# Output pieces of a soft-MoE kernel through two DMA queues: the column halves alternate between SyncE and GpSimd

## The chip, the cores and the metric

The kernel runs on one core of a Trainium2 chip. The metric is the device time of one execution in microseconds (us), as the median over several runs. A core has five engines with instruction streams of their own: TensorE (PE, with its weight loads as PEld), VectorE (DVE), ScalarE (ACT), GpSimd (POOL) and SyncE (SP). Data between HBM and the on-chip memory goes through 16 DMA engines, which all DMA queues share. A profile is taken of one execution and has times in us from the start of its span.

## The reference

Sliding-window causal attention (window 64) feeds a soft mixture of experts with 8 experts of 4 slots. There are 8 batches of 576 tokens, 8 heads of 64, so D = 512 and the output has 4608 rows of 512 float32 values.

```python
scores = scale * np.matmul(q, k.transpose(0, 1, 3, 2))      # q, k, v: (8, 8, 576, 64)
scores = np.where((rel >= 0) & (rel < 64), scores, -1e9)
x = softmax(scores) @ v                                      # -> (4608, 512)
logits = x @ phi                                             # (4608, 32)
slot_input = softmax(logits, axis=0).T @ x                   # 32 slots
slot_out[e] = np.maximum(slot_input[e] @ w1[e], 0) @ w2[e]   # F = 1024
out = softmax(logits, axis=1) @ slot_out                     # (4608, 512) float32
```

## The kernel before

For the first 150 us the kernel works through 32 pairs of heads in a software pipeline written out by hand: scores, exponentials, the product with V, the router's logits, and running sums of the slots' inputs. Loads of q, k, v and of the experts' weights are issued by GpSimd, which also converts them from float32 to float16 on the way; they go through queue q0 of the profile ("software_dynamic"). SP issues the first few loads and all outputs, through queue q1 ("hardware_dynamic").

From 151 us on the experts run. `first` and `turn_hidden` make the hidden values, `second` and `second_last` multiply by the second weights, one half of the 512 columns at a time (`DH` = 256): `osb` has its columns 0 to 255 at 159.9 us and its columns 256 to 511 at 165.1 us. The last weights come in by column halves as well (`load_half`, lines 148 to 156).

The output is 8 x 576 rows. Two batches make a group `k` (0 to 3) of 1,152 rows, which is laid out as 128 partitions of `NE` = 9 neighbouring rows each (`e` = 0 to 8). `give(k, e0, ne, c0, nc_)` (lines 883 to 902) makes one piece, `ne` rows per partition and `nc_` columns from `c0`. It multiplies the spread weights `ct4[k]` by the slots' outputs `osb` into a PSUM tile `cp` (line 893), divides by the sums while it copies to SBUF, by DVE (line 898) or ACT (line 900) in turn, and issues one DMA to HBM (line 902). A whole-row piece has 3 x 512 neighbouring values in a partition, one packet of 6 KB; a piece of a column half has `ne` packets of 1 KB in each partition.

The pieces lie in seven SBUF buffers `obs` that once held the first experts' weights. A piece takes the next buffer in turn, so piece i can be written only after piece i-7 has landed. The order of pieces is written out in lines 909 to 938: the two halves of group 0 and of the first three rows of group 1 first (8 pieces of 256, 256, 640, 384, 256, 384, 512 and 384 KB), then 8 pieces of whole rows with 768 KB each. Every engine executes its own instructions in the order written, so a DMA that waits for its data holds up the ones behind it on the same engine.

Of the kernel before, what the change touches and what calls it, by code (L numbers as in the profile page):

```python
# [18 lines left out]
def kernel(  # L19
# [10 lines left out]
    nc = tc.nc  # L30
# [115 lines left out]
    DH = D // 2  # L146
# [507 lines left out]
    def spread(b, copy, rp=None):  # L654
        if rp is None:
            rp = psr.tile([128, 1024], FP32, name="rp", tag="rp")
        for t in range(5):
            w = 128 if t < 4 else 64
            nc.tensor.matmul(rp[:, 128 * t:128 * t + w], ss4[:, min(t, 3), :],
                             ct_all[:, b, 128 * (t // 4):128 * (t // 4) + w], start=True, stop=True,  # L660
                             skip_group_check=True)
        copy(out=ct4[b // 2][:, :, 64 * (b % 2):64 * (b % 2) + 64],
             in_=rp[:, 0:S].rearrange("p (x e) -> p e x", e=NE))
# [170 lines left out]
    def second(d, g, js=range(4)):  # L834
        for fc in range(NFC):
            for j in js:
                nc.tensor.matmul(ops[d][32 * j:32 * j + 32, 0:DH], hT[g][:, fc, 32 * j:32 * j + 32],
                                 w2_at(4 * g + j, d, fc), start=(g == 0 and fc == 0), stop=False,
                                 skip_group_check=True)
# [40 lines left out]

    turn, piece = 0, 0

    def give(k, e0, ne, c0, nc_):
        nonlocal turn, piece
        ov = out[2 * S * k:2 * S * k + 2 * S, :].rearrange("(p e) d -> p e d", e=NE)
        ob = obs[piece % NRES][:, 0:ne * nc_].rearrange("p (e d) -> p e d", d=nc_)
        piece += 1
        n1 = 512 // nc_
        for i0 in range(0, ne, n1):
            n_ = min(n1, ne - i0)  # L890
            cp = pst.tile([128, n1, nc_], FP32, name="cp", tag="cp")
            for i in range(n_):
                nc.tensor.matmul(cp[:, i, :], ct4[k][:, e0 + i0 + i, :], osb[:, c0:c0 + nc_],  # L893
                                 start=True, stop=True, skip_group_check=True)
            for i in range(n_):
                rc = rcs[:, k, e0 + i0 + i:e0 + i0 + i + 1]
                if turn % 2:
                    nc.vector.tensor_scalar(out=ob[:, i0 + i, :], in0=cp[:, i, :], scalar1=rc, scalar2=None, op0=ALU.mult)  # L898
                else:
                    nc.scalar.activation(ob[:, i0 + i, :], cp[:, i, :], AF.Copy, scale=rc)  # L900
            turn += 1
        nc.sync.dma_start(out=ov[:, e0:e0 + ne, c0:c0 + nc_], in_=ob)

    def spread_product(b):
        rp = psr.tile([128, 1024], FP32, name="rp", tag="rp")
# [5 lines left out]
    late = []  # L911
    spread_product(3)
    give(0, 0, 2, 0, DH)
    give(0, 2, 2, 0, DH)
    dve(out=late[0][0], in_=late[0][1])
    give(0, 4, 5, 0, DH)
    second(1, 0)
    second(1, 1, (0, 1))
    sums(1)
# [1 line left out]
    second_last(1)  # L921
    act(out=osb[:, DH:D], in_=ops[1][:, 0:DH])
    give(0, 0, 2, DH, DH)
    give(0, 2, 3, DH, DH)
    give(0, 5, 4, DH, DH)
    spread(4, act)
    give(1, 0, 3, DH, DH)
    spread(5, dve)
    for k in range(1, B // 2):
        for e0 in range(3 if k == 1 else 0, NE, 3):  # L930
# [36 lines left out]
```

## Time and profile before

| | |
|---|---|
| Median of 3 runs | 190.65 us (190.38 to 191.93) |
| The profiled execution | 192.31 us, span 190.5 us |
| Busy share of the span | PE 85%, PEld 64%, DVE 75%, ACT 76%, POOL 52% |
| Output | 9.44 MB in 16 DMAs, all issued by SP |
| First and last output issue | 161.3 us, 178.3 us |

PE is the busiest engine over the whole span. In the last fifth the picture is another one: the compute engines end near 177.6 us while the DMA engines work on. In the stretch tables, the columns behind an engine's busy time give its instructions (x), then come the clock granted to TensorE, the DMA share (the mean of the 16 engines; it can pass 1 where packets overlap) and GB/s. GB/s counts what is written, so a load that converts to float16 shows half of what it reads. In the DMA views each queue has a line with packets, MB and the time its packets took as a share of 16 engines' time.

### The profile page before, as it was taken

Reading aid. Unit: us, or ns where it says so; the run is one execution under the profiler, and the core shown is the slowest. Engines: PE = TensorE matmul, PEld = TensorE weight load, DVE = VectorE, ACT = ScalarE, POOL = GpSimd, SP = SyncE. Lnnn points to the kernel's source line nnn. Section 1 sums busy time; section 2 is a strip of 40 time slices with the busy share of each in tenths; the row PEclk is TensorE's granted clock in tenths of the full one; section 3 lists DMA queues with packets and bytes.
Section 4 is the critical chain, followed back from the end, with each engine's and each line's share of the span. In section 5 each row is a group of like instructions: output and inputs, shape, how many; then the busy total and the mean of one; then the engine's idle time right before and its main releaser. Section 6 shows DMA issues by size and latency. Waiting matters only on the chain.

```text
span 190.5 us, 7073 instructions
## 1 busy us (share of the span) xinstructions
PE 162.3 (85%) x3039; PEld 121.6 (64%) x3039; DVE 142.7 (75%) x354; ACT 145.1 (76%) x267; POOL 98.8 (52%) x123
## 2 busy tenths in 40 slices
PE   5987999999999999999999899999988898878100
PEld 1566878877777777777777787776774466643000
DVE  6778686897778789788888988888886555699400
ACT  6558979989889899888998898988588257499200
POOL 7956937274696644973984828736844160000000
PEclk9999999999999999999999999999999999999955
DMA  6999999999999999999999999999999999999993
GB/s 171 207 185 189 224 177 220 179 224 178 186 222 178 216 187 185 211 194 182 214 187 202 202 184 203 196 200 201 214 212 212 201 196 154 310 341 415 413 410 125
DMA packets 62303, 41.48 MB, mean 218 GB/s; under 512 B 38848, under 2 KB 58304, under 8 KB 61376
## 3 DMA queue, kind: packets, MB, share of 16 engines
q0 software_dynamic: 56560, 30.35, 115.4%
q1 hardware_dynamic: 5712, 10.68, 15.8%
q8 instruction: 24, 0.39, 0.7%
q14 instruction: 7, 0.06, 0.1%
HBM read 61.93 MB, written 9.44 MB: 375 GB/s over the span
## 4 chain that ended last, share of the span: by engine, by line
PE 44%; DVE 26%; issue 7%; ACT 7%; DMA 4%; POOL 4%; DVEq 0%; ACTq 0%; POOLq 0%
DVE m L353 7%; PE a_m L346 5%; PE a_m L349 5%; DVE x_b L415 4%; PE a_q L316 4%; PE a_s L372 3%; PE a_v L405 3%; PE a_s L375 3%; DMA out_dram<-w 3%; PE a_k L316 2%; DVE acc L526 2%; DVE kT L324 2%; PE a_k L429 2%; PE ha L816 2%; DVE rt L367 2%
## 5 line engine op out<-in xcount | busy, mean ns | idle before, releaser
L336 ACT ACTIVATE qb<-a_q 64x576 f16<-64x576 f16 x63 | 40.6, 645 | 6.9 <-PE a_q L316 5.4
L353 DVE TENSOR_REDUCE m<-a_m 128x8 f16<-128x1024 f32 x32 | 39.1, 1223 | 1.9 <-PE a_m L349 1.0
L381 ACT ACTIVATE pt<-a_s 128x1024 f16<-128x1024 f32 x32 | 32.8, 1025 | 6.8 <-PE a_s L375 5.5
L180 POOL COPY v<-v 64x1152 f16<-64x1152 f16 x16 | 18.3, 1142 | 33.3 <-DMA v<-in_v_dram 32.0
L415 DVE TENSOR_TENSOR x_b<-a_v,rc 128x640 f16<-128x640 f32 x31 | 25.6, 825 | 1.1
L349 PEld LDWEIGHTS <-qb 128*128 128x128 f16 x256 | 17.3, 99 | 8.5 <-ACT qb L336 0.8
L349 PE MATMUL a_m<-kT,qb 128*128 128x128 f16 x256 | 20.0, 222 | 0.3 <-ACT qb L336 0.3
L375 PEld LDWEIGHTS <-lh 128*128 128x128 f16 x288 | 18.7, 98 | 2.0 <-issue 1.7
L173 POOL DMA_DIRECT2D v<-in_v_dram x16 | 20.0, 1247 | 0.0
L346 PE MATMUL a_m<-wm,ident_h 128*128 128x512 f16 x64 | 19.8, 391 | 0.2 <-DVE m L353 0.2
L372 PEld LDWEIGHTS <-kT 128*128 128x128 f16 x288 | 18.6, 98 | 1.6 <-issue 1.4
L433 ACT COPY xt<-a_k 128x576 f16<-128x576 f16 x28 | 17.9, 640 | 2.2 <-PE a_k L429 0.9
L372 PE MATMUL a_s<-qb,kT 128*128 128x128 f16 x256 | 19.5, 219 | 0.0
L375 PE MATMUL a_s<-rt,lh 128*128 128x128 f16 x256 | 19.5, 219 | 0.0
L182 POOL COPY v<-v 64x1088 f16<-64x1088 f16 (+1 forms) x16 | 17.9, 1119 | 0.8
L405 PE MATMUL a_v<-v,pt 128*64 128x65 f16 x558 | 15.8, 196 | 2.5 <-DVE m L363 1.1
L367 DVE CAST rt<-a_v 9x128 f16<-9x128 f32 x30 | 8.7, 289 | 10.8 <-PE a_v L366 10.5
L405 PEld LDWEIGHTS <-pt 128*64 128x64 f16 x576 | 13.6, 110 | 4.9 <-issue 1.8
L79 POOL DMA_DIRECT2D ks<-in_k_dram x15 | 10.7, 714 | 11.0 <-DMA w<-in_moe_w_dram 3.9
L327 ACT ACTIVATE kT<-a_k 128x576 f16<-128x576 f16 x24 | 15.7, 654 | 0.8 <-PE a_k L316 0.8
L316 PE MATMUL a_q<-ident_h,qs 96*64 96x96 f16 x384 | 15.2, 211 | 1.2 <-DVE a_q L225 1.0
L898 DVE TENSOR_SCALAR w<-cp,rcs 128x256 f32<-128x256 f32 (+1 forms) x24 | 13.5, 611 | 2.1 <-PE cp L893 1.7
(183 smaller groups left out, 332.8 us busy)
## 6 DMA issues: line engine op xcount, KB each, us to landing
w<-in_moe_w_dram POOLq DMA_DIRECT2D x13, 1024.0 KB, 16.8
out_dram<-w SPq DMA_DIRECT2D x8, 768.0 KB, 7.7
v<-in_v_dram POOLq DMA_DIRECT2D x16, 288.0 KB, 12.5
ks<-in_k_dram POOLq DMA_DIRECT2D x15, 288.0 KB, 15.4
qs<-in_q_dram POOLq DMA_DIRECT2D x15, 288.0 KB, 12.6
out_dram<-w SPq DMA_DIRECT2D x3, 384.0 KB, 3.5
w1h<-in_moe_w_dram POOLq DMA_DIRECT2D x4, 256.0 KB, 16.1
w<-in_moe_w_dram POOLq DMA_DIRECT2D x4, 256.0 KB, 14.9
```

The source lines that it names most:

```text
L173: nc.gpsimd.dma_start(out=v1s[b % 2][:, c, 0:Dh], in_=v[b].rearrange("h s d -> (h s) d").rearrange("(c p) d -> p c d", p=128)[:, c, :])
L180: nc.gpsimd.tensor_copy(out=v2[64:128, c0:c1, 0:Dh], in_=v1[0:64, c0:c1, 0:Dh])
L316: nc.tensor.transpose(tq[64 * hf:64 * hf + 64, RP * r:RP * r + RP], src[0:RP, h + hf, Dh * r:Dh * r + Dh], ident_h[0:RP, 0:RP])
L336: nc.scalar.activation(qbs[p % NQ][h, :, hf, :], turned(a_qh)[h], AF.Copy, scale=QKS)
L346: nc.tensor.matmul(a_m[:, j, :], ident_h[:, :], wm[:, j:j + 4, :].rearrange("p c x -> p (c x)"), start=True, stop=False, skip_group_check= ...
L349: nc.tensor.matmul(a_m[:, i // 4, 128 * (i % 4):128 * (i % 4) + 128], qblock(p, i), kwindow(p, i), start=False, stop=True, skip_group_chec ...
L353: nc.vector.reduce_max(ms[p % 2][:, 64:72].rearrange("p (l c) -> p l c", l=2), a_m[:, :, :].rearrange("p l (c x) -> p l c x", x=128), axis ...
L372: nc.tensor.matmul(at(i), kwindow(p, i), qblock(p, i), start=(i % 4 == 0), stop=False, skip_group_check=True)
L375: nc.tensor.matmul(at(i), lh[:, i, :], rt[:, :], start=False, stop=True, skip_group_check=True)
L381: nc.scalar.activation(st_pt(p)[:, 0:8, :].rearrange("p i x -> p (i x)"), a_s[:, :, :], AF.Exp, scale=XS)
L405: nc.tensor.matmul(a_v[r0:r0 + 64, hf, 65 * (i // 2):65 * (i // 2) + 65], pt[:, i, 64 * hf:64 * hf + 64], rhs, start=True, stop=True, skip ...
L415: nc.vector.tensor_tensor(out=xbs[b][:, :, 128 * hp:128 * hp + 128].rearrange("p c (l d) -> p l c d", l=2), in0=avv[:, :, :, 0:64], in1=rc ...
```

## The change

`give` gets a parameter for the engine that issues its DMA, SP unless told otherwise. Of the pieces of column halves, every second one goes through GpSimd. The piece of five rows (group 0, rows 4 to 8, first columns) becomes two pieces of 2 and 3 rows, so there are 9 pieces of column halves in place of 8: five through SP and four through GpSimd. The piece of group 1 in the first columns, which the diff does not show, stays on SP. All pieces of whole rows stay on SP.

```diff
-    def give(k, e0, ne, c0, nc_):
+    def give(k, e0, ne, c0, nc_, queue=nc.sync):
...
-        nc.sync.dma_start(out=ov[:, e0:e0 + ne, c0:c0 + nc_], in_=ob)
+        queue.dma_start(out=ov[:, e0:e0 + ne, c0:c0 + nc_], in_=ob)
...
     give(0, 0, 2, 0, DH)
-    give(0, 2, 2, 0, DH)
+    give(0, 2, 2, 0, DH, nc.gpsimd)
     dve(out=late[0][0], in_=late[0][1])
-    give(0, 4, 5, 0, DH)
+    give(0, 4, 2, 0, DH)
+    give(0, 6, 3, 0, DH, nc.gpsimd)
     second(1, 0)
...
     give(0, 0, 2, DH, DH)
-    give(0, 2, 3, DH, DH)
+    give(0, 2, 3, DH, DH, nc.gpsimd)
     give(0, 5, 4, DH, DH)
     spread(4, act)
-    give(1, 0, 3, DH, DH)
+    give(1, 0, 3, DH, DH, nc.gpsimd)
     spread(5, dve)
```

## The prediction

> **What bounds the kernel now.** I read the page's slices first, then the stretch from the first output piece to the end by stretches, then that stretch's DMA queues, then the lines of the issuing engines. The slices show the DMA engines at 9 to the end while every compute engine falls off after slice 36:
>
> ```profile
> PE   5987999999999999999999899999988898878100
> ...
> DMA  6999999999999999999999999999999999999993
> ```
>
> ```profile
> core 0: us, PE busy (x) PEld busy (x) DVE busy (x) ACT busy (x) POOL busy (x), PEclk, DMA share, GB/s
> ...
> 163.75:164.00 0.25, 0.25 (x3) 0.04 (x1) 0.22 (x1) 0.00 (x0) 0.00 (x0) 1.00 0.70 215
> 164.00:165.75 1.75, 1.28 (x23) 1.07 (x23) 1.11 (x3) 0.86 (x3) 0.00 (x0) 1.00 1.05 354
> 165.75:166.00 0.25, 0.25 (x3) 0.10 (x1) 0.25 (x2) 0.25 (x1) 0.00 (x0) 1.00 0.69 225
> 167.00:167.50 0.50, 0.41 (x5) 0.21 (x3) 0.50 (x2) 0.50 (x2) 0.00 (x0) 1.00 0.82 275
> ...
> 172.50:181.00 8.50, 4.18 (x27) 1.45 (x25) 5.57 (x10) 4.52 (x8) 0.00 (x0) 1.00 1.02 413
> ...
> 187.25:189.00 1.75, 0.00 (x0) 0.00 (x0) 0.00 (x0) 0.00 (x0) 0.00 (x0) 0.50 0.06 25
> ```
>
> The last two columns are read here. A full DMA share goes with 354 GB/s while the column halves go out (rows of 1 KB) and with 413 GB/s for whole rows (6 KB). Over 16 engines that is 46.3 ns for a 1 KB packet and 238 ns for a 6 KB one (39.7 ns per KB). Compute ends at 177.6, yet data moves until 189: the tail is DMA-bound. The engines run dry three times before 167.5, for (0.30 + 0.31) x 0.25 + 0.18 x 0.5 = 0.24 us of a mean engine. And the last row is one engine of 16 (0.06): fifteen are done at 187.25, one works 1.75 us longer. Why it lags stands in the DMA views of 163 to 164.5 and of 181 to 183, one line of each:
>
> ```profile
> q8 instruction: 1, 0.02, 4.0%
> ```
>
> ```profile
> q8 instruction: 1, 0.02, 2.9%
> ```
>
> Two instruction fetches, 4.0% of 16 x 1.5 and 2.9% of 16 x 2 engine-us, are 0.96 and 0.93 us, 1.89 together, about the lag less the gaps that the others had. That both fell on the same engine is inferred from that sum. I call it the late engine: **it sets the end**, and what the other fifteen lose costs nothing until they are later than it is.
>
> **Issue, and who could be late.** For the 16 issues, line 902:
>
> ```profile
> L902 SPq DMA_DIRECT2D out_dram<-w x16: 332/404/1133, 161.3 to 178.3; - x16
> ...
> DMA to landing us min/median/max: 2.8/4.6/11.1
> ```
>
> Asked by single microseconds they start at 161.3, 161.8, 163.0, 165.0, 166.4, 166.9, 167.8 and 168.6 (halves), then 169.8 to 178.3 (whole rows). The last lands 11.1 us after its issue, so supply is some 8 us ahead at the end: a whole piece is 786 KB, 1.9 us at 413 GB/s. SP's 0.4 us a piece therefore buys nothing late. GpSimd is idle in this stretch; its last work is
>
> ```profile
> 155.85 0.51 POOL L488 TENSOR_TENSOR lh<-lh,nm 128x192 f32<-128x192 f32 x1 [0.21 <-DVE nm L483]
> ```
>
> **The change, part by part.** In the built program's order every matmul and eviction keeps its place and engine (the split piece had evictions of 2, 2 and 1 rows, and has them still). Only buffer numbers shift by one after the split. SP has 13 output DMAs in place of 16; GpSimd gets four at its end: pieces of 2, 3, 3 and 3 rows, 11 x 128 = 1,408 packets of 1 KB, 88 to a DMA engine. Nothing stands behind them on GpSimd; their own semaphores were last used by loads issued before 146, landed by 159.
>
> *Issue time.* SP drops four issues and gains one: 3 x 0.4 = 1.2 us of an engine that waits anyway. A GpSimd issue of 512 rows (line 155) takes
>
> ```profile
> L155 POOL DMA_DIRECT2D w2h<-in_moe_w_dram x4: 742/742/742, 143.9 to 153.9; - x4
> ```
>
> so 4 x 0.74 us on an idle engine. Both cost 0, covered by the data in flight.
>
> *Time per packet.* No row shows a GpSimd store. Nearest by what moves is SP's own 1 KB store, 46.3 ns. GpSimd's loads of 1 KB rows (halved to 512 B) at 153 to 157 were 1,574 packets less 48 small ones in 4 us: 41.9 ns. Their time in flight, 144.8% of 64 engine-us over 1,574, is 58.9 ns. On 88 packets the bounds are -4.4 x 88 = -0.39 us and +12.6 x 88 = +1.11 us. I take the store's row: 0.
>
> *Delay to the first packet.* SP: issue at 161.27, first packet just after 162.1, 0.9 us. GpSimd on an empty ring is seen once, at the kernel's start: issue at 2.05, only SP's packets until 5.3, first two of its own by 5.6, some 3.3 us. Between 0.9 and 3.3 I take 3.3, since SP's ring was then as full as now. The second piece (evicted at 161.45) would start at 164.8 instead of 163, the fourth (162.9) at 166.2. SP's two pieces of 2 rows, the second now issued near 162.1, last until about 163.8 as before. The gap there grows from 0.25 to 1 us, and 0.3 us follow before 165.95. A common engine loses (1.0 + 0.3) - 0.24, about 1.1 us: it ends near 188.3, not 187.25. But the late engine spends one gap on its first fetch (it lags 0.96 us there) and starves for 0.1 to 0.3 us at most. With 0.9 us instead, it starves for nothing. I take **+0.1 us**. Were that cover gone (no fetch there), the 1.1 us would all show.
>
> *Buffers.* With seven buffers, piece i (from 0) waits for the landing of i-7. Pieces 13 and 15 (k=2 e0=6, k=3 e0=3) now wait for GpSimd's third and fourth. Issued at 166.9 and 168.6, with 3.3 us of delay and 1.1 us of data each, these land near 172 and 174; the two pieces are issued at 174.9 and 177.0 in the trace, after 1.4 us of evictions, so their buffers are wanted near 173.5 and 175.5. Cost 0, if the rings share so that 1.1 us of data takes no more than a few.
>
> *Sum.* The profiled execution: 192.31 us, span 190.5, 1.8 around it. 192.31 + 0 + 0 + 0.1 + 0 = 192.4. It is 1.66 above the median of the runs shown, so **190.8 us** against 190.65.
>
> The Trainium skill, "DMA: Bandwidth & Descriptors", section "Issuing engines are not separate DMA queues", says that DMAs from sync, scalar and GpSimd end on the same 16 engines and that more issuers save issue time alone. By that rule the sum is the same, 0 for bandwidth; the shares of 1.05 and 1.02 with one issuer agree.
>
> **Rivals.**
>
> *Slower: the last GpSimd piece lands too late.* Its 24 packets per engine meet SP's 6 KB packets. Shared packet by packet, each costs 46 + 238 = 284 ns. For: at 5 to 9 us, where both rings were full, GpSimd moved 625 packets and SP 675, near one to one. Against: at 162.25 to 163.25 GpSimd's load tail ran on at 145 packets beside SP's 219, about the rate it had alone on the few engines that still held it. One to one, the third piece (from 170.2) has some 16 packets beside 6 KB ones, 4.5 us, and ends at 175; the fourth needs 24 x 0.284 = 6.8 us more: 182, on the late engine 183 to 184. Who waits is piece 15: eviction of three rows on two engines, 2 x 0.68, then 0.9 us to data. The late engine has finished piece 14 at 189.0 - 2 x 1.9 = 185.2, so the landing decides from 182.9 on, and then us for us: 0.1 to 1.1 late, and with the third piece's own delay to piece 13 up to 3. I price it at +1.7: **192.4 us**.
>
> The Trainium skill, "DMA: Bandwidth & Descriptors", section "Queues, rings and completion order", has each DMA engine go round its rings, a packet of about 9 to 17 descriptors at a time. By that an estimate is 24 descriptors in two or three turns, each behind a turn of SP's of up to a whole piece, 1.9 us: 5 to 7 us, much as one to one. It speaks for this rival, and so do the counts at 5 to 9 us; those at 162.25 do not.
>
> *Dearer packets.* GpSimd's store packets cost their time in flight: +1.1 on the late engine, with 0.3 of starving: **192.1 us**. For: the 58.9 ns. Against: they overlap, 41.9 ns apart.
>
> *Faster: two rings fill each other's gaps.* All 24 x 8 = 192 packets of 1 KB on an engine fall from 46.3 to 39.7 ns: -1.27 us, **189.4 us**. For: the share of 1.19 with both rings at 162.25 to 163.25. Against: that stretch moved 364 packets in a us, 44 ns each, little better than one ring.
>
> **How the numbers follow.** Forecast 0.50, late landing 0.25, dearer packets 0.12, filled gaps 0.13. The likeliest's own range is 190.2 to 191.6. A change of 1%, 1.9 us, is about what a measurement of this kernel can tell from none. Slower by more: half of the late landing, a third of the dearer packets, and some for both together with a cost that no row shows, 0.25. Faster by more needs -1.9, past the -1.27 and -0.39 worked out; I leave 0.12, mostly for a late engine that lags less. Same: 0.63. The range is 189.3 to 193.2.
>
> **What would show it.** Right: data until 188.8 to 189.4, one engine alone for the last 0.6 us or more, SP's half-row rate still near 354, GpSimd's pieces landing within 6 us, a hole in the DMA share near 164 to 165. Wrong: GpSimd's fourth piece landing after 182, with DVE or ACT waiting for it at line 898 or 900 and DMA share under 1 at 183 to 186; or more than 370 GB/s with both rings at work.

## The result and the profile after

Over 22 runs each, the changed kernel took 191.75 us in the median (191.19 to 193.16), the kernel before 190.88 us (190.38 to 192.11). The ratio is 1.0052 with a 95% interval of 1.0031 to 1.0072: **slower by 0.5%**, about 0.9 us. The forecast was 190.8, and its range (189.3 to 193.2) holds the time, which lies just above the likeliest outcome's own range (190.2 to 191.6). But the loss is clear of noise, and it is most of an amount that the prediction had worked out and then set aside. The profiled execution has a span of 191.1 us.

Counted from the first output issue, the compute engines did what they did before, to within 0.2 us; the two profiles of the kernel before (e12 below is the second) differ by as much. What changed is the DMA stretch between the first output issue (161.0) and 172. Here it is in stretches (the last two columns are DMA share and GB/s):

```profile
core 0: us, PE busy (x) PEld busy (x) DVE busy (x) ACT busy (x) POOL busy (x), PEclk, DMA share, GB/s
163.75:164.25 0.50, 0.50 (x13) 0.32 (x13) 0.43 (x2) 0.39 (x1) 0.23 (x1) 1.00 0.96 326
164.25:164.75 0.50, 0.30 (x7) 0.19 (x4) 0.44 (x2) 0.21 (x2) 0.00 (x0) 1.00 0.75 252
164.75:166.75 2.00, 1.28 (x12) 1.01 (x12) 1.27 (x3) 1.31 (x4) 0.00 (x0) 1.00 1.01 366
166.75:167.25 0.50, 0.50 (x9) 0.40 (x7) 0.44 (x2) 0.50 (x3) 0.00 (x0) 1.00 0.47 156
167.25:168.00 0.75, 0.28 (x5) 0.17 (x4) 0.75 (x3) 0.75 (x2) 0.72 (x1) 1.00 1.01 344
168.00:168.75 0.75, 0.75 (x8) 0.27 (x5) 0.55 (x2) 0.72 (x3) 0.06 (x1) 1.00 0.37 128
168.75:171.25 2.50, 2.05 (x19) 0.94 (x19) 2.50 (x6) 2.32 (x4) 0.76 (x1) 1.00 1.00 333
171.25:171.75 0.50, 0.50 (x8) 0.33 (x6) 0.50 (x1) 0.42 (x1) 0.00 (x0) 1.00 0.94 309
174.00:187.00 13.00, 2.83 (x14) 0.73 (x10) 4.01 (x7) 3.28 (x6) 0.00 (x0) 0.78 1.01 412
...
188.00:189.25 1.25, 0.00 (x0) 0.00 (x0) 0.00 (x0) 0.00 (x0) 0.00 (x0) 0.50 0.07 29
```

The full stretches run at the rates of before: 412 GB/s for whole rows (413 before), 333 to 366 for column halves. But there are holes: 0.25 x 0.5 + 0.53 x 0.5 + 0.63 x 0.75 + 0.06 x 0.5 = 0.89 us of a mean engine, against 0.24 before. The largest, at 168.0 to 168.75, did not exist. Before, the same stretch was full:

```profile
168.00:168.75 0.75, 0.75 (x8) 0.33 (x6) 0.55 (x2) 0.75 (x3) 0.00 (x0) 1.00 1.03 335
```

GpSimd's four issues show why (its timeline from 160 on):

```profile
161.49 0.73 POOL L902 DMA_DIRECT2D out_dram<-w  x1 [5.42 <-DVE w L898]
163.22 0.77 POOL L902 DMA_DIRECT2D out_dram<-w  x1 [0.99 <-DVE w L898]
167.28 0.78 POOL L902 DMA_DIRECT2D out_dram<-w  x1 [3.30 <-ACT w L900]
168.81 0.76 POOL L902 DMA_DIRECT2D out_dram<-w  x1 [0.75 <-ACT w L900]
```

The third is issued at 167.28, and at 168.5 to 168.65 queue q0 moves its first packet, some 1.4 us after the issue (1.36 to 1.37 in each of the four traces that have this hole: this one, e5, e7 and e9); SP's first output packet came 0.9 us after its issue. On top, the issue itself is late. Before, SP issued this piece 5.6 us after the first output issue; GpSimd does it 6.3 us after. Of these 0.6 us, 0.2 are a later compute (the next piece of SP is 0.2 late as well), the rest is GpSimd's own: it issues 0.3 us (first and fourth piece) to 0.6 us (second and third) after the last eviction of the piece, SP within 0.1 us when it is free.

One thing of the queue table was in no account: GpSimd does not send the rows as SP does.

```profile
q0 software_dynamic: 56976, 31.79, 117.2%
q1 hardware_dynamic: 4256, 9.24, 13.6%
```

Before:

```profile
q0 software_dynamic: 56560, 30.35, 115.4%
q1 hardware_dynamic: 5712, 10.68, 15.8%
```

SP has lost 1,456, which is 1,408 rows and 3 x 16 completions. GpSimd has gained 416, which is 4 x 16 completions and 352 packets: four rows of 1 KB in each, 1.44 MB in all.

### The profile page after: what moved, and what is told of

Same layout as the page of the kernel before. It is cut to its first block, busy times and chain, and to the rows that moved or that the text cites. A ratio compares the mean times of both kernels' runs of the same rounds, so it can differ in the third digit from the quotient of the medians.

```text
span 191.1 us, 7073 instructions
## 1 busy us (share of the span) xinstructions
PE 162.1 (85%) x3039; PEld 121.4 (64%) x3039; DVE 143.1 (75%) x354; ACT 145.0 (76%) x267; POOL 101.2 (53%) x127
## 4 chain that ended last, share of the span: by engine, by line
PE 47%; DVE 33%; ACT 7%; issue 4%; DMA 2%; DVEq 0%; SPq 0%; ACTq 0%
DVE m L353 10%; PE a_m L346 6%; PE a_m L349 5%; DVE x_b L415 5%; PE a_s L372 4%; PE a_s L375 4%; PE a_v L405 3%; PE a_q L316 3%; DVE acc L526 3%; PE a_k L429 2%; DVE kT L324 2%; DVE rt L367 2%; DMA w<-in_q_dram 2%; PE ha L816 2%; PE op L837 2%
## 5 line engine op out<-in xcount | busy, mean ns | idle before, releaser
L405 PE MATMUL a_v<-v,pt 128*64 128x65 f16 x558 | 15.3, 196 | 2.2 <-DVE m L363 1.1
```

Source lines behind the costliest of these rows:

```text
L405: nc.tensor.matmul(a_v[r0:r0 + 64, hf, 65 * (i // 2):65 * (i // 2) + 65], pt[:, i, 64 * hf:64 * hf + 64], rhs, start=True, stop=True, skip ...
```

## The experiments

**Theory A**: GpSimd's pieces reach the DMA engines later than SP's; where little else waits the engines run dry, and a DMA-bound tail never makes that up. **Theory B**: DMA time itself grows, by a second ring or by GpSimd's packets. **Theory C**: the split costs it. Each experiment but e12, a single run, was timed beside the kernel before. In the table, "gap" is summed over the quarter microseconds from 1 to 25 us after the first output issue with a DMA share under 0.95 (what is missing to 1; a packet counts in each quarter with the part that lies in it), and "end" is when, after that issue, the share falls under a half. Both come from one profile of each kernel.

| Kernel | Ratio to before (95%) | Gap, us | End, us |
|---|---|---|---|
| before, two profiles | 1 | 0.23; 0.26 | 26.0; 26.25 |
| changed, first profile | 1.0052 (1.0031 to 1.0072) | 1.04 | 26.75 |
| e5, changed again | 1.0044 (1.0008 to 1.0079) | 1.07 | 26.75 |
| e1, split, all on SP | 0.9988 (0.9953 to 1.0022) | 0.49 | 26.0 |
| e2, ACT for GpSimd | 1.0002 (0.9971 to 1.0033) | 0.36 | 26.25 |
| e3, before + 768 KB | 1.0076 (1.0049 to 1.0103) | 0.24 | 28.0 |
| e4, changed + 768 KB | 1.0098 (1.0065 to 1.0132) | 0.07 | 27.75 |
| e6, first two on GpSimd | 0.9988 (0.9958 to 1.0018) | 0.37 | 26.0 |
| e7, last two on GpSimd | 1.0104 (1.0058 to 1.0150) | 1.16 | 26.75 |
| e8, whole rows on GpSimd | 1.0020 (0.9987 to 1.0054) | 0.41 | 26.25 |
| e9, the third alone | 1.0042 (1.0009 to 1.0075) | 0.97 | 26.5 |
| e10, the fourth alone | 1.0011 (0.9985 to 1.0036) | 0.37 | 26.0 |
| e11, all but the third | 1.0019 (0.9992 to 1.0046) | 0.42 | 26.25 |

**e1: the split alone.**

```diff
-    give(0, 2, 2, 0, DH, nc.gpsimd)
+    give(0, 2, 2, 0, DH)
...
-    give(0, 6, 3, 0, DH, nc.gpsimd)
+    give(0, 6, 3, 0, DH)
...
```

and the other two back on SP in the same way.

> The changed kernel with its split piece, but every piece issued by SP. Theory A (GpSimd's pieces reach the DMA engines later than SP's, and the gaps that this opens before 169 us, while there is nothing else to send, are never made up): the split alone opens no gap and closes the one at 163.75, so 0 to -0.3 us against before (190.6 to 190.9). Theory B (a second ring, or GpSimd's packets, cost DMA time): also 0, since neither is used. Theory C (the split, with one DMA more and the buffers moved by one, costs the time): +0.6 to +0.9 us, as the change.

Measured: 191.27 us in the median, 191.04 before, ratio 0.9988 (0.9953 to 1.0022). Theory C falls: its +0.6 us would be 1.003. One expectation missed: the split does open a gap, 0.34 us at 5.25 to 6.5 us after the first issue (0.10 and 0.16 in the two profiles of before), but the end and the time do not show it.

**e2: ACT in GpSimd's place.**

```diff
-    give(0, 2, 2, 0, DH, nc.gpsimd)
+    give(0, 2, 2, 0, DH, nc.scalar)
...
```

> The changed kernel with ACT in GpSimd's place: the same four pieces, a second ring, but issued by an engine like SP. Theory A: first packets about 0.9 us after the issue as with SP, no new gap beyond what ACT's four issues of 0.4 us take from its evictions: -0.2 to +0.4 us against before. Theory B as a cost of two rings: +0.6 to +0.9 us. Theory B as a cost of GpSimd's packets alone: as A.

Measured: 190.94 us, ratio 1.0002 (0.9971 to 1.0033). The four pieces went through a ring of their own, q10, as packets of 1 KB, and nothing was lost. So a second ring costs nothing that shows here, and wins nothing either. What is left of theory B is GpSimd's packets.

**e3 and e4: a cushion of work.** Both kernels get the same addition behind the first piece:

```diff
     give(0, 0, 2, 0, DH)
+    o3 = out[6 * S:8 * S, :].rearrange("(p e) d -> p e d", e=NE)
+    for e in range(3):
+        nc.sync.dma_start(out=o3[:, e, :], in_=w1_t[e, 0][:, 3, :].bitcast(FP32))
```

> The kernel before with 768 KB more to send: right behind the first piece SP issues three DMAs of 256 KB from SBUF to output rows that later pieces write anew. Both theories: 1.9 us more of DMA work at 413 GB/s, less the 0.24 us of gaps that it fills: +1.6 to +1.9 us against before, with no share under 0.95 between 163 and 187 us.

> The changed kernel with the same 768 KB behind its first piece, so that the DMA engines have work while GpSimd's pieces are on their way. Theory A: the gaps (1.03 us of a mean engine in the changed kernel's trace, against 0.24 before) are filled, and the difference to the kernel before with the same addition is within 0.3 us. Theory B (DMA time itself has grown): the difference stays at +0.6 to +0.9 us.

Measured: 192.92 and 192.89 us, ratios 1.0076 and 1.0098. The two intervals overlap widely (the ratios differ by 0.2%, 0.4 us, with some 0.8 us of uncertainty), so the times alone do not decide. The traces speak for theory A. In e4, the stretch with the three holes is full:

```profile
163.00:169.00 6.00, 4.42 (x56) 2.83 (x55) 4.48 (x11) 4.27 (x10) 1.86 (x3) 1.00 1.04 362
...
168.00:168.75 0.75, 0.75 (x6) 0.15 (x3) 0.60 (x1) 0.72 (x3) 0.06 (x1) 1.00 1.02 354
```

and its engines end 27.75 us after the first issue, 28.0 in e3. With the holes filled, 1.44 MB through GpSimd take no more DMA time than through SP. The 1.5 to 2 us that both lose to before are the added 1.9 us. One expectation for e3 missed: it kept a gap of 0.24 us, with a share as low as 0.53, at 3.0 to 3.75 us after its first issue; there SP took 1.6 us to issue the last of the three added DMAs (0.4 us in e4), and what stood behind it came late.

**e5: the changed kernel again.**

> The changed kernel itself once more, for a second profile beside the others of this group and for its time on their chip. Theory A (GpSimd's pieces start late and open gaps that are not made up; in the executions where no DMA engine is held up by an instruction fetch in the tail, all of this shows): +0.6 to +1.0 us against before, gaps of about 1 us of a mean engine between 163 and 172 us, and if no fetch falls in the tail, all engines done within 0.3 us of each other, 26.5 to 27 us after the first issue. Theory B (DMA time itself has grown): the same time, but the rate in the full stretches below that of before.

Measured: 191.81 us, ratio 1.0044 (1.0008 to 1.0079). The large hole is there again, in its own trace at 168.6 to 169.25, and the full stretch goes at the old rate. This time no engine is left over at the end:

```profile
168.60:169.25 0.65, 0.65 (x8) 0.38 (x7) 0.44 (x2) 0.62 (x3) 0.16 (x1) 0.95 0.31 102
...
176.00:187.00 11.00, 1.57 (x5) 0.38 (x4) 2.92 (x5) 1.99 (x4) 0.00 (x0) 0.70 1.02 415
188.00:188.50 0.50, 0.00 (x0) 0.00 (x0) 0.00 (x0) 0.00 (x0) 0.00 (x0) 0.50 0.78 320
188.50:188.75 0.25, 0.00 (x0) 0.00 (x0) 0.00 (x0) 0.00 (x0) 0.00 (x0) 0.50 0.02 0
```

This matters for the prediction, below.

**e6 and e7: half of the pieces each.** In e6 the pieces of the first column half stay on GpSimd and the others return to SP; in e7 the other way round.

> Only the first two of the four pieces (256 and 384 KB, columns 0 to 255 of group 0) go through GpSimd, with the split; the other two are back on SP. Theory A: a gap near 164.5 of some 0.15 us and the one near 167 that the split alone has too, but not the 0.5 us near 168.3: 0 to +0.4 us against before. Theory B: cost in proportion to the bytes, 5 of 11 rows: +0.3 to +0.4 us, with a lower rate.

> Only the last two of the four pieces (384 KB each, columns 256 to 511) go through GpSimd, with the split; the first two are back on SP. Theory A: the gap of some 0.5 us near 168.3 stays and that near 164.5 goes: +0.4 to +0.9 us against before, most of the change's cost. Theory B: 6 of 11 rows, +0.4 to +0.5 us.

Measured: 190.98 us, ratio 0.9988, and 193.26 us, ratio 1.0104. Theory B wanted the cost shared about evenly; whatever can be told from noise is with the second pair. e7 is even dearer than the change itself, more than theory A said (+0.4 to +0.9 us). Its gap, 1.16 us, is hardly larger than the change's (1.04 and 1.07); its profile has the late engine described below, 1.5 us behind the others. Whether that is in all of its runs isn't known; what of its +2 us comes from there stays open.

**e8: GpSimd where SP is ahead.** On the kernel before, with the new parameter of `give`:

```diff
-            give(k, e0, 3, 0, D)
+            give(k, e0, 3, 0, D, nc.gpsimd if (k, e0) in ((1, 6), (2, 3), (3, 0)) else nc.sync)
```

> The kernel before, with three of the eight whole-row pieces (group 1 rows 6 to 8, group 2 rows 3 to 5, group 3 rows 0 to 2) through GpSimd and all column halves on SP. There SP has 2 to 8 us of data waiting. Theory A: GpSimd's later start is covered, no gap, 0 to +0.3 us against before, though GpSimd carries 2.36 MB and not 1.44. Theory B: DMA time in proportion to GpSimd's bytes, +1.0 to +1.5 us, with 380 GB/s or less where both rings work.

Measured: 191.41 us, ratio 1.0020 (0.9987 to 1.0054). More bytes (2.36 MB) through GpSimd than in the change, and a loss that can't be told from none. GpSimd's first packet left at 174.1, 2.1 us after its issue at 172.04, yet with SP's data waiting the gaps from 9 us after the first output issue on add up to 0.05 us. From 172 to 178 both rings together moved 404 GB/s:

```profile
q1 hardware_dynamic: 350, 1.64, 68.7%
q0 software_dynamic: 136, 0.79, 32.7%
```

**e9, e10 and e11: one DMA.** e9 and e10 are the kernel before with one DMA moved to GpSimd, e11 the changed kernel with that of e9 moved back. e9:

```diff
-    give(0, 2, 3, DH, DH)
+    give(0, 2, 3, DH, DH, nc.gpsimd)
```

e10:

```diff
-    give(1, 0, 3, DH, DH)
+    give(1, 0, 3, DH, DH, nc.gpsimd)
```

> The kernel before with one DMA alone moved to GpSimd, group 0 rows 2 to 4 in the second column half (384 KB, the piece that the changed kernel issues at 167.3). SP has only 256 KB before it and nothing behind it until 167.8. Theory A: the gap near 168.3, 0.4 to 0.6 us of a mean engine, comes back with this one DMA, and the time rises by as much: +0.3 to +0.7 us. Theory B (cost by GpSimd's bytes): 3 rows of 11, +0.2 us, no gap.

> The kernel before with one DMA alone moved to GpSimd, group 1 rows 0 to 2 in the second column half (384 KB as well, issued near 168.7). SP has 512 KB waiting before it and whole rows soon behind it. Theory A: the same delay of the first packet, but covered but for 0.1 us: 0 to +0.2 us. Theory B: as its twin, +0.2 us.

> The changed kernel with that one DMA (group 0 rows 2 to 4, second half) back on SP; the other three stay on GpSimd. Theory A: the gap near 168.3 is gone, some 0.4 to 0.6 us are left over the span from 163 to 172 us, and the time is within 0.3 us of before. Theory B: 8 rows of 11 stay, +0.5 to +0.6 us.

Measured: 191.61 us, ratio 1.0042; 191.56 us, ratio 1.0011; 191.35 us, ratio 1.0019, with before at 191.12. One DMA of 384 KB costs as much as the whole change did in e5, its twin 1.5 us later nothing that shows, and without it the change has no loss that can be told from noise. Against each other the times of e9 and e10 do not decide: the ratios differ by 0.3%, with some 0.4% of uncertainty, and the medians by 0.05 us. What decides is that time and trace go together: the four kernels whose traces have the hole near 168 to 169 (the change, e5, e7, e9) have ratios of 1.0042 to 1.0104, the six without it (e1, e2, e6, e8, e10, e11) of 0.9988 to 1.0020. The hole in e9:

```profile
168.30:168.50 0.20, 0.13 (x3) 0.13 (x3) 0.20 (x1) 0.20 (x2) 0.20 (x1) 1.00 1.05 348
168.50:169.25 0.75, 0.75 (x8) 0.31 (x6) 0.55 (x2) 0.75 (x3) 0.14 (x1) 1.00 0.24 82
169.25:169.50 0.25, 0.18 (x1) 0.00 (x0) 0.25 (x2) 0.25 (x1) 0.00 (x0) 1.00 1.08 377
```

and the issue that opens it, in GpSimd's timeline:

```profile
167.87 0.77 POOL L902 DMA_DIRECT2D out_dram<-w  x1 [11.02 <-ACT w L900]
```

That is 6.1 us after e9's first output issue; in the first profile of before SP issued the piece 5.6 us after, all other issues but the last standing alike to 0.1 us. So GpSimd issues it 0.5 us later although it did nothing else for 11 us, and its packets start just before 169.25, some 1.4 us after the issue. Piece 0.5 later, packets another 0.5 later: about 1 us, of which the hole is 0.76 x 0.75 = 0.57.

**e12: the kernel before, one look.**

> The kernel before once more, for a second profile. If no instruction fetch falls into the time after 175 us, all DMA engines end within 0.3 us of each other, about 26.0 to 26.3 us after the first output issue, though a fetch near 163 is there; then the late engine of the first profile owes its 1.7 us to the fetch in the tail alone. If one engine is still 0.9 us late with only the early fetch, the prediction's account of the late engine stands.

Measured: one run, 189.91 us, span 188.1. All engines end together, 26.25 us after the first issue:

```profile
186.00:186.50 0.50, 0.00 (x0) 0.00 (x0) 0.00 (x0) 0.00 (x0) 0.00 (x0) 0.50 0.87 356
186.50:186.75 0.25, 0.00 (x0) 0.00 (x0) 0.00 (x0) 0.00 (x0) 0.00 (x0) 0.50 0.03 0
```

No experiment came out clearly faster than before; the best ratios, 0.9988 for e1 and e6, have 1 in their intervals.

## Why the prediction was right, and where it was not

The range held the time, but not by the account behind the forecast. That account allowed 0.1 us, and 0.9 us came; the range was wide because of rivals that did not happen. That part is luck.

*The bound.* Right. From the first issue the DMA engines set the time, and what is lost there shows at the end. Gap and end go together through the table: up to 0.5 us of gap, end at 26.0 to 26.25; about 1 us, end at 26.5 to 26.75 (the two kernels with added work aside).

*Issue time, time per packet.* Right: 0 and 0. The row that stood for GpSimd's packets was one of 1 KB, and they hold 4 KB, but e4 shows the same DMA time.

*Delay to the first packet.* The mechanism is the one named, a later start that opens gaps while supply is thin, and the common engine's loss was put at 1.1 us; the traces show 0.65 to 0.8 us more gap than before, of which some 0.6 is seen at the last packet. Its parts were off. The delay of GpSimd's third piece is 1.4 us after the issue, not 3.3; added to that are 0.6 us between the last eviction and the issue, which the prediction had not. The Trainium skill, "DMA: Bandwidth & Descriptors", section "Specifications", gives about 1 us to the first byte for GpSimd's DMAs and about 0.6 for SP's. The measured values, counted from the start of the issue, are 1.4 and 0.9: both larger, but their difference of 0.5 us is close to the page's 0.4, far closer than the 2.4 us that the kernel's cold start had suggested. And the costly place was not the second and fourth piece but the seventh (piece 6, GpSimd's third), which the prediction followed only for its buffer. The gap predicted at 164 to 165 was there, the smallest of the three that count (0.13 us).

*The late engine: the step that failed.* The prediction set the 1.1 us aside as covered by one late engine and took +0.1. The cover was not there. In e5 and e12 the fetch near 163 is in the trace as before, one 16 KB packet at 162 to 164 in e12:

```profile
q8 instruction: 1, 0.02, 2.7%
```

yet all engines end together there; what is missing is the second fetch, in the tail. So the lag of the first profile came from the tail fetch alone, though its packet took only 0.93 us. It comes after the gaps, at 181 to 183, and cannot hide them. Of the profiles here, those with the tail fetch (the first of before, the first of the change, e1, e7, e9) end 1.5 to 1.8 us later on one engine, those without end together within 0.4 us. With the cover, the lag would have shrunk as the gaps grew; it is 1.65 us in the change and 1.5 in e7, with gaps of 1.04 and 1.16, against 1.75 before with 0.23. Why the early fetch leaves no lag, and why the tail fetch leaves more than its own 0.93 us, stays open. The change's cost is alike in both: last packet 27.7 against 28.4 us after the first issue with the fetch, 26.25 against 26.8 without. Nor does the change only meet the tail fetch more often: the shortest of its 22 runs is 0.8 us longer than the shortest of the 22 before (191.19 against 190.38). An inference from a sum, 0.96 + 0.93 being near 1.75, carried the forecast, and the second profile of the same kernel was what undid it. The signs that the prediction had named for being right were all there in the changed kernel's trace: data until 189.4, one engine alone at the end, half rows at 333 to 366 GB/s, GpSimd's pieces landing within 6 us, a hole at 164 to 165. As stated, none of them could tell a covered gap from an uncovered one; the size of the lag could: 1.65 us, where the prediction's own numbers leave 1.75 + 0.1 - 1.1, some 0.75.

*Buffers, and the rival of the late landing.* Its sharing was right and its price wrong. Where both rings were full, at 172 to 173.5, they moved packet for packet:

```profile
q1 hardware_dynamic: 56, 0.34, 58.5%
q0 software_dynamic: 57, 0.22, 40.6%
```

But GpSimd's packets hold four rows, so its last piece needs 6 turns per engine, not 24, and its data was through by 174, long before 182.9. The Trainium skill, "DMA: Bandwidth & Descriptors", section "Queues, rings and completion order", has turns of about 9 to 17 descriptors. Such turns do not show here: 56 packets went against 57, and the 96 packets of GpSimd's last piece all began within 2.4 us (171.4 to 173.8), where six turns of one packet each from both rings are 6 x (0.19 + 0.24) = 2.6 us. The Trainium skill, same page, section "SWDGE vs HWDGE vs iDMA", has packets hold preferably 4,096 bytes at most, and a DMA engine change rings between packets. The 352 packets of 4 KB agree with it; in e8, whose rows of whole pieces are 6 KB, GpSimd's 384 packets hold 6 KB each.

*Dearer packets, filled gaps.* Neither: the ends of e4 and e3 (27.75 and 28.0 us) leave no room for a growth of +1.1 us in DMA time, and the stretches with both rings moved 366 GB/s (164.75 to 166.75) and 374 (172 to 173.5, with 6 KB packets on one of them), little above the 354 of SP's column halves alone. The prediction's sign for filled gaps, over 370, is met by the second, but there the 6 KB packets account for it (413 GB/s alone).

## What to carry to other kernels

In a DMA-bound tail, bytes and rates are only half of the account; the other half is whether the engines ever run dry, and there the start-up delay of an issue counts unless other data already waits. Before moving a DMA to a queue that starts later, look at what else is queued at that very moment: here one DMA of 384 KB opened the hole and cost about as much as the whole change, and its twin 1.5 us later opened none and cost nothing that shows. And do not let a forecast lean on slack seen in one profile; whether one late engine is a fixture or a chance event takes a second profile to tell.

## What the runs showed of the hardware

A DMA of 1 KB rows from SBUF that GpSimd issued went out in 4 KB packets (352 for 1,408 rows), one that SP or ACT issued in 1 KB packets; a 4 KB packet took about 188 ns and a 1 KB packet 46 to 48 ns, so the rate was about the same. GpSimd's first packet came 1.4 us after the start of the issue where the engines ran dry (the change, e5, e7, e9) and 2.1 us after it where SP's data was in the rings (e8, e10); SP's first came 0.9 us after. An instruction fetch of 16 KB in the tail, with a packet time of 0.88 to 0.96 us, left one DMA engine 1.5 to 1.8 us behind the others, and it fell into the tail in some executions of a program and not in others: the changed program once with it (last packet 28.4 us after the first issue) and once without (26.8).
